# Attention's 1/rms: eleven VectorE operations for two tiles, or a GpSimd power for each tile

## The chip, the cores and the metric

The kernel runs on one core of a Trainium2 chip. Its engines work side by side, each through its own list of instructions in order: TensorE (PE, matrix products and transposes; its weight loads are PEld), VectorE (DVE), ScalarE (ACT), GpSimd (POOL) and SyncE (SP, which only starts DMA transfers). An instruction that needs another engine's result waits at the head of its list, and everything behind it on that engine waits too. The metric is the device time of one execution in microseconds (us): 1328.89 in the median of three runs of the kernel before.

## The reference

Three stages in a row, all in float32, on 8 batches of 576 tokens (4608 in all) and 512 features (8 heads of 64).

```python
kv  = einsum('bhsd,bhse->bhde', k, v)                  # 64 x 64 for each batch and head
out = einsum('bhsd,bhde->bhse', q, kv)
rms = sqrt(mean(out * out, axis=-1, keepdims=True) + 1e-06)   # over the 64 of one head
x   = out / rms * g_norm                               # tokens x 512

h = x @ w_in;   x = (h * cos(h)) @ w_out               # 512 -> 2048 -> 512

h = x @ w_in2                                          # 512 -> 1024
e = exp(h - max(h));  solu = h * e / (sum(e) + 1e-09)
ln = (solu - mean(solu)) / sqrt(var(solu) + 1e-06) * g_ln
out = ln @ w_out2                                      # 1024 -> 512
```

## The kernel before

**Stages.** Attention is cut into 36 tiles of 128 tokens by 512 features. It runs inside the first of four passes over the first feed-forward block: each pass takes 4 of the 16 chunks of 128 hidden features, and goes through 9 blocks of 512 tokens, so a pass has 36 steps. A step multiplies a block of x by one chunk of `w_in` (bank ps_h, lines 174 to 176 from `step_h`), applies h times cos(h) on ACT and DVE, and multiplies by a chunk of `w_out` (banks ps_acc, the same three lines from `step_out`). Each product is done as three products of rounded high and low parts. After the four passes comes the second block. The weights arrive as words of 64 bits and are brought into float32 on the chip (`convert`, `split_w`: lines 500 to 527), most of that on DVE.

**One attention tile.** PE multiplies q by kv (line 416, `first`); ACT squares the result (line 421); DVE sums the squares over each head to 128 x 8 numbers (line 422). Once both tiles of a pair have their sums, DVE makes 1/rms of all 16 columns in eleven small operations (`newton`: a first guess from the bits of the number, then three Newton steps; lines 429 to 440). DVE scales each tile by it (line 458, below called the norm), PE turns the tile by four transposes (line 463, below the turn), and ACT copies the turned tile to x with g_norm (line 469). The products k by v (lines 358 and 360) for the next batches stand between these. The first of a pair's norms therefore waits for the second tile's product, square and sum.

**Order.** The program isn't run in the order in which it is written. `Flow` records every operation as a task with an engine, a duration in us written into the source, the tiles it reads and writes, and a wished time `at`; `run` then plans the engines' lists from these. An engine takes the task with the least `at` among those that could start first; tasks of POOL, and those of DVE that don't have `ps=True`, are planned one at a time (`port`). So another duration or another engine for one task moves others on every engine. The tasks after an attention product have `at` lowered by `PRI`, 20 us, and so go ahead of others when they are ready.

**Other POOL work.** POOL makes the low parts of x (line 569, from block 3 on; DVE does the first three blocks) and of the weights of the later passes (line 527; DVE does those of the first), and in the last stage a power of one column for each tile (line 756):

```python
add("POOL", 0.56, lambda: POOL.tensor_tensor(out=sm("ry"), in0=sm("v"), in1=buf["mhalf"][:, 0:1], op=ALU.pow),
```

Of the kernel before, what the change touches and what calls it, by code (L numbers as in the profile page):

```python
# [10 lines left out]
I32 = mybir.dt.int32  # L11
# [30 lines left out]
MAGIC = float(0x5F3759DF)  # L42

TINY = 0.17
# [18 lines left out]
class Flow:  # L63
# [13 lines left out]
    def declare(self, pool, tag, n, shape, dt=F32):  # L77

        for key in [(tag, i) for i in range(n)] if n else [tag]:
            self.pool_of[key] = pool  # L80
            self.specs.setdefault(pool, []).append((key, shape, dt))
# [18 lines left out]
    def add(self, eng, dur, fn, r=(), w=(), at=0.0, lat=0.0, ps=False):  # L100
        t = Task()
        t.eng, t.dur, t.fn, t.at, t.lat = eng, dur, fn, at, lat
        t.port = eng == "POOL" or (eng == "DVE" and not ps)
# [52 lines left out]
def tile_kernel(ctx, tc, qkv, tail, g2, w1, w2, gl, out):  # L156
# [33 lines left out]
    declare("const", "mhalf", 0, [P, 1])  # L190
# [29 lines left out]
    for n in ("ss", "y", "yt"):  # L220
        declare("att", n, 2, [P, 2 * H])
# [104 lines left out]
    def stage():  # L326
        n_st[0] += 1
        return "st", (n_st[0] - 1) % NST
# [64 lines left out]
    def tile_slots(g):  # L393


        i = g % 2
        bks = [next_bank() for _ in range(2)]
        ss, y, yt = ("ss", i), ("y", i), ("yt", i)
        halves = [("ssh", g, h) for h in range(2)]

        def heads(ap):
            return ap.rearrange("p (n w) -> p n w", w=D)

        def first(h, at):
            t, bk, sq = 2 * g + h, bks[h], stage()
            for b, a, n, row in parts(t):
# [6 lines left out]
                def mm(b=b, a=a, n=n, row=row, qs=qs, kvf=kvf):  # L413
                    for p in range(NPAIR):
# [6 lines left out]
            add("ACT", 0.61, lambda: ACT.activation(out=buf[sq], in_=buf[bk], func=AF.Square), r=[bk], w=[sq], at=at)  # L421
            add("DVE", 0.66, lambda: DVE.tensor_reduce(out=buf[ss][:, h * H:(h + 1) * H], in_=heads(buf[sq]), axis=AX.X,
                                                       op=ALU.add), r=[sq] + ([ss] if h else []),
                w=[halves[h]] + ([] if h else [ss]), at=at)


        def newton(at):
            def start():
                DVE.tensor_scalar(out=buf[ss], in0=buf[ss], scalar1=1.0 / D, scalar2=1e-6, op0=ALU.mult, op1=ALU.add)
                DVE.tensor_scalar(out=buf[y].bitcast(I32), in0=buf[ss].bitcast(I32), scalar1=-0.5, scalar2=MAGIC,  # L430
                                  op0=ALU.mult, op1=ALU.add)

            def square():
                DVE.tensor_tensor(out=buf[yt], in0=buf[y], in1=buf[y], op=ALU.mult)  # L434

            def times():
                DVE.scalar_tensor_tensor(out=buf[yt], in0=buf[yt], scalar=-0.5, in1=buf[ss], op0=ALU.mult, op1=ALU.mult)  # L437

            def update():
                DVE.scalar_tensor_tensor(out=buf[y], in0=buf[yt], scalar=1.5, in1=buf[y], op0=ALU.add, op1=ALU.mult)  # L440

            def all_():
                start()
                for _ in range(3):
                    square()
                    times()
                    update()

            add("DVE", 11 * TINY, all_, r=[*halves, ss], w=[ss, y, yt], at=at)

        def second_(h, at):
            t, bk, xn = 2 * g + h, bks[h], ("xn", h)
# [4 lines left out]
            def norm():  # L457
                DVE.tensor_tensor(out=heads(buf[xn]), in0=heads(buf[bk]),
                                  in1=buf[y][:, h * H:(h + 1) * H].unsqueeze(2).to_broadcast([P, H, D]), op=ALU.mult)
# [7 lines left out]
            add("DVE", 0.71, norm, r=[bk, y], w=[xn], at=at, ps=True)  # L467
# [4 lines left out]
        def run0(at):  # L472
            first(0, at)

        def run1(at):
            first(1, at)
            newton(at - PRI)
            for h in range(2):
                second_(h, at - PRI)

        return [run0, run1]
# [382 lines left out]
    def slot(ps_, c):  # L864
        return ps_ % 2 * CPP + c
# [134 lines left out]
```

## Time and profile before

| | |
|---|---|
| three runs | 1328.19, 1328.89, 1331.12 us; median 1328.89 |
| the profiled execution | 1329.38 us; 1327.6 us from its first to its last instruction |
| busy over that span | PE 98%, DVE 70%, ACT 51%, POOL 29% |
| granted TensorE clock, mean | 0.992 |

The profile is one execution. In its rows a line such as L463 is line 463 of the kernel; an operation is written out<-in by the tiles' names, without buffer numbers; "x4" is four instructions merged, and a merged row's time runs from the first start to the last end. What stands in brackets at a row's end is idle time of the engine before it, and the operation that ended it. PE's busy time holds overlapping matmuls whose ends are modelled. A matmul on float32 operands (lines 358, 360 and 416) shows as two instructions in the trace, and as one in the listings of the program's order.

### The profile page before, as it was taken

How to read it: one execution, taken by the hardware profiler on the slowest of the kernel's cores; microseconds unless marked ns; L12 is line 12 of the kernel's file. 1: busy time of each engine (PE TensorE's matmuls, PEld its weight loads, DVE VectorE, ACT ScalarE, POOL GpSimd, SP SyncE). 2: the span in 40 equal slices, each digit the busy share in tenths (PEclk: the TensorE clock that was granted, in tenths of full speed). 3: DMA queues.
4: the chain of work that ended last, by engine and by line, in shares of the span. 5: the costliest groups of instructions: out<-in, count | busy, mean ns of one | idle time of the engine just before them, and what ended most of it. 6: DMA issues, size and time to landing. Idle time of an engine off the chain costs nothing.

```text
span 1327.6 us, 17232 instructions
## 1 busy us (share of the span) xinstructions
PE 1295.1 (98%) x6148; PEld 1077.8 (81%) x6148; DVE 927.8 (70%) x1620; ACT 676.7 (51%) x1195; POOL 385.6 (29%) x364
## 2 busy tenths in 40 slices
PE   6789899999999999999999999999999999999998
PEld 6678788888888888888888888888788888888886
DVE  5889556588986456754545677878987878787853
ACT  3556445467655445545444555555554544444432
POOL 0001212036663225523131456443232212121100
PEclk9899999999999999999999999999999999999999
DMA  8643244323544243423232535464110111010000
GB/s 299 206 140 115 84 147 131 101 96 96 171 146 135 72 119 113 149 68 123 79 112 87 151 109 159 142 213 137 67 46 35 56 56 46 35 56 25 16 32 32
DMA packets 61830, 139.54 MB, mean 105 GB/s; under 512 B 7344, under 2 KB 9392, under 8 KB 60592
## 3 DMA queue, kind: packets, MB, share of 16 engines
q1 hardware_dynamic: 61744, 138.44, 32.4%
q8 instruction: 48, 0.79, 0.2%
q14 instruction: 38, 0.31, 0.1%
HBM read 91.23 MB, written 47.19 MB: 104 GB/s over the span
## 4 chain that ended last, share of the span: by engine, by line
PE 86%; DVE 6%; DMA 3%; ACT 2%; issue 1%; SPq 0%; POOL 0%; ACTq 0%; DVEq 0%
PE ps_acc L176 13%; PE ps_acc L174 13%; PE ps_acc L175 13%; PE ps_h L174 13%; PE ps_h L176 12%; PE ps_h L175 12%; PE ps_acc L773 2%; PE ps_o L416 2%; PE ps_o L358 2%; DMA xt<-w 2%; PE ps_o L463 1%; DVE att L440 1%; DVE att L437 1%; DVE att L434 1%; DMA xt<-qkv 1%
## 5 line engine op out<-in xcount | busy, mean ns | idle before, releaser
L569 POOL TENSOR_TENSOR xhl<-xt,xhl 128x512 fp32r<-128x512 f32 (+3 forms) x176 | 191.6, 1118 | 360.1 <-ACT xhl L564 359.9
L174 PE MATMUL ps_acc<-temps,wpool 128*128 128x512 f32 x648 | 254.5, 393 | 0.0
L176 PE MATMUL ps_acc<-temps,wpool 128*128 128x512 f32 x648 | 252.5, 390 | 0.0
L175 PE MATMUL ps_acc<-temps,wpool 128*128 128x512 f32 x648 | 252.5, 390 | 0.0
L174 PE MATMUL ps_h<-xhl,wpool 128*128 128x512 f32 x576 | 227.0, 394 | 0.5 <-ACT xhl L564 0.3
L175 PE MATMUL ps_h<-xhl,wpool 128*128 128x512 f32 x576 | 224.6, 390 | 0.2 <-DVE xhl L569 0.2
L176 PE MATMUL ps_h<-xhl,wpool 128*128 128x512 f32 x576 | 224.5, 390 | 0.0
L594 DVE SCALAR_TENSOR_TENSOR temps<-ps_h,temps 128x512 f32<-128x512 f32 x144 | 99.1, 688 | 112.3 <-ACT temps L592 111.8
L603 DVE TENSOR_TENSOR temps<-temps,temps 128x512 fp32r<-128x512 f32 x144 | 122.1, 848 | 69.7 <-ACT temps L602 69.0
L597 ACT ACTIVATE temps<-temps,const 128x512 f32<-128x512 f32 x144 | 104.2, 724 | 94.4 <-DVE temps L594 94.2
L592 ACT ACTIVATE temps<-ps_h 128x512 int32<-128x512 f32 x144 | 85.8, 596 | 129.0 <-PE ps_h L176 128.1
L600 DVE TENSOR_TENSOR temps<-ps_h,temps 128x512 f32<-128x512 f32 x144 | 99.0, 687 | 65.5 <-ACT temps L597 65.3
L176 PEld LDWEIGHTS ps_acc<-temps,wpool 128*128 128x128 f32 x648 | 121.8, 188 | 25.5
L174 PEld LDWEIGHTS ps_acc<-temps,wpool 128*128 128x128 f32 x648 | 122.0, 188 | 24.9 <-DVE temps L630 0.3
L175 PEld LDWEIGHTS ps_acc<-temps,wpool 128*128 128x128 f32 x648 | 121.9, 188 | 24.6
L602 ACT CAST temps<-temps 128x512 fp32r<-128x512 f32 x144 | 89.4, 621 | 100.2 <-DVE temps L600 90.9
L174 PEld LDWEIGHTS ps_h<-xhl,wpool 128*128 128x128 f32 x576 | 108.3, 188 | 23.4 <-issue 0.7
L176 PEld LDWEIGHTS ps_h<-xhl,wpool 128*128 128x128 f32 x576 | 108.2, 188 | 22.6
L175 PEld LDWEIGHTS ps_h<-xhl,wpool 128*128 128x128 f32 x576 | 108.4, 188 | 22.2 <-DVE xhl L569 0.5
L564 ACT CAST xhl<-xt 128x512 fp32r<-128x512 f32 (+3 forms) x192 | 90.8, 512 | 12.8 <-PE ps_h L176 11.9
L756 POOL TENSOR_TENSOR xt<-xt,const 128x1 f32<-128x1 f32 x36 | 23.0, 638 | 196.8 <-DVE xt L753 189.3
L779 DVE TENSOR_TENSOR wpool<-ps_acc,wpool 128x512 fp32r<-128x512 f32 x72 | 46.6, 686 | 42.6 <-ACT wpool L776 42.6
(140 smaller groups left out, 2259.2 us busy)
## 6 DMA issues: line engine op xcount, KB each, us to landing
px<-temps SPq DMA_DIRECT2D x144, 256.0 KB, 2.6
temps<-px SPq DMA_DIRECT2D x108, 256.0 KB, 3.9
xt<-w SPq DMA_DIRECT2D x28, 512.0 KB, 3.9
att<-qkv SPq DMA_DIRECT2D x24, 512.0 KB, 4.7
rawp<-w SPq DMA_DIRECT2D x20, 512.0 KB, 3.8
xt<-px SPq DMA_DIRECT2D x9, 1024.0 KB, 5.1
out<-temps SPq DMA_DIRECT2D x36, 256.0 KB, 2.0
att<-qkv SPq DMA_DIRECT2D x28, 288.0 KB, 5.3
```

Source lines behind the costliest of these rows:

```text
L174: PE.matmul(ps, lhsT=lh, rhs=rh, start=start, stop=False)
L175: PE.matmul(ps, lhsT=lh, rhs=rl, start=False, stop=False)
L176: PE.matmul(ps, lhsT=ll, rhs=rh, start=False, stop=stop)
L564: ACT.copy(out=buf["xh", i][:, k, a - m * TB:a - m * TB + n], in_=xt(k, a, n))
L569: eng.tensor_tensor(out=buf["xl", i][:, k, r], in0=xt(k, a, n), in1=f(buf["xh", i][:, k, r]), op=ALU.subtract)
L592: add("ACT", 0.61, lambda: ACT.activation(out=buf["kk"], in_=h(), func=AF.Copy, scale=INV_2PI, bias=0.25), r=[hb], w=["kk"], at=at)
L594: add("DVE", 0.71, lambda: DVE.scalar_tensor_tensor(out=buf[tk], in0=h(), scalar=INV_2PI, in1=buf["kk"], op0=ALU.mult, op1=ALU.subtract), ...
L597: add("ACT", 0.74, lambda: ACT.activation(out=buf[tk], in_=buf[tk], func=AF.Sin, bias=buf["halfpi"][:, 0:1], scale=2 * math.pi), r=[tk, "h ...
L600: add("DVE", 0.71, lambda: DVE.tensor_tensor(out=buf[tk], in0=h(), in1=buf[tk], op=ALU.mult), r=[hb, tk], w=[tk], at=at, ps=True)
L602: add("ACT", 0.64, lambda: ACT.copy(out=buf[ghk], in_=buf[tk]), r=[tk], w=[ghk], at=at + 2)
L603: add("DVE", 0.71, lambda: DVE.tensor_tensor(out=buf[glk], in0=buf[tk], in1=f(buf[ghk]), op=ALU.subtract), r=[tk, ghk], w=[glk], at=at + 2)
L779: DVE.tensor_tensor(out=buf["ll", n][:, part, :], in0=tr(), in1=f(buf["lh", n][:, part, :]), op=ALU.subtract)
```

## The change

1/rms is made tile by tile, on POOL, by two instructions on 128 x 8 numbers: the sum of squares plus 1e-6, and that to the power -0.5 (a tensor of -0.5 as exponent, `mhalf`, now with 8 columns). The division by 64 goes into the square's scale on ACT. The buffers `ss` and `y` are four of 8 columns instead of two of 16, `yt` goes. A tile's task `rms` is planned with 2.0 us on POOL and outside the one-at-a-time rule; a tile's norm and turn now depend on that tile alone. Lines further down move up by up to 21: the turn is line 443 after the change, the norm 438, the sum 419, the q by kv products 412, the two POOL instructions 426 and 427.

```diff
--- before.py
+++ after.py
@@ -39,9 +39,8 @@
 XP = NT // NX
 
 INV_2PI = float(1.0 / (2.0 * math.pi))
-MAGIC = float(0x5F3759DF)
-
-TINY = 0.17
+
+POW = 2.0
 
 
 
@@ -100,7 +99,7 @@
     def add(self, eng, dur, fn, r=(), w=(), at=0.0, lat=0.0, ps=False):
         t = Task()
         t.eng, t.dur, t.fn, t.at, t.lat = eng, dur, fn, at, lat
-        t.port = eng == "POOL" or (eng == "DVE" and not ps)
+        t.port = eng in ("POOL", "DVE") and not ps
         t.deps, t.next, t.end, t.left, t.seq = set(), [], None, 0, len(self.tasks)
         for k in {*r, *(self.pool_of[k] for k in (*r, *w) if k in self.pool_of)}:
             if k in self.writer:
@@ -187,7 +186,7 @@
     px2 = dram.tile([NB, P, KC, TB], F32, name="px2")
     for key in ("g2", "halfpi"):
         declare("const", key, 0, [P, 1])
-    declare("const", "mhalf", 0, [P, 1])
+    declare("const", "mhalf", 0, [P, H])
     declare("const", "gl", 0, [P, NC])
     declare("const", "ident", 0, [P, P])
 
@@ -217,8 +216,8 @@
         declare(pool, "q" + i, n_q, [P, S])
     declare("att", "kvf", 2, [P, DM])
     declare("att", "xn", 2, [P, DM])
-    for n in ("ss", "y", "yt"):
-        declare("att", n, 2, [P, 2 * H])
+    for n in ("ss", "y"):
+        declare("att", n, 4, [P, H])
 
     for pool, i, n_st, n_y, n_f in (("spare1", "a", 2, 2, 2), ("rawp", "b", 2, 2, 2), ("late_x0", "c", 1, 1, 6)):
         declare(pool, "wst" + i, n_st, [P, 512, 2], U32)
@@ -393,16 +392,13 @@
     def tile_slots(g):
 
 
-        i = g % 2
         bks = [next_bank() for _ in range(2)]
-        ss, y, yt = ("ss", i), ("y", i), ("yt", i)
-        halves = [("ssh", g, h) for h in range(2)]
 
         def heads(ap):
             return ap.rearrange("p (n w) -> p n w", w=D)
 
         def first(h, at):
-            t, bk, sq = 2 * g + h, bks[h], stage()
+            t, i, bk, sq = 2 * g + h, (2 * g + h) % 4, bks[h], stage()
             for b, a, n, row in parts(t):
                 qs = [key("q", b * NPAIR + p, 6, 3) for p in range(NPAIR)]
                 kvf = ("kvf", b % 2)
@@ -418,45 +414,29 @@
 
                 add("PE", 0.89, mm, r=[kvf, ("kvfh", kvf, 0), ("kvfh", kvf, 1), *qs], w=[bk], at=at)
             at -= PRI
-            add("ACT", 0.61, lambda: ACT.activation(out=buf[sq], in_=buf[bk], func=AF.Square), r=[bk], w=[sq], at=at)
-            add("DVE", 0.66, lambda: DVE.tensor_reduce(out=buf[ss][:, h * H:(h + 1) * H], in_=heads(buf[sq]), axis=AX.X,
-                                                       op=ALU.add), r=[sq] + ([ss] if h else []),
-                w=[halves[h]] + ([] if h else [ss]), at=at)
-
-
-        def newton(at):
-            def start():
-                DVE.tensor_scalar(out=buf[ss], in0=buf[ss], scalar1=1.0 / D, scalar2=1e-6, op0=ALU.mult, op1=ALU.add)
-                DVE.tensor_scalar(out=buf[y].bitcast(I32), in0=buf[ss].bitcast(I32), scalar1=-0.5, scalar2=MAGIC,
-                                  op0=ALU.mult, op1=ALU.add)
-
-            def square():
-                DVE.tensor_tensor(out=buf[yt], in0=buf[y], in1=buf[y], op=ALU.mult)
-
-            def times():
-                DVE.scalar_tensor_tensor(out=buf[yt], in0=buf[yt], scalar=-0.5, in1=buf[ss], op0=ALU.mult, op1=ALU.mult)
-
-            def update():
-                DVE.scalar_tensor_tensor(out=buf[y], in0=buf[yt], scalar=1.5, in1=buf[y], op0=ALU.add, op1=ALU.mult)
-
-            def all_():
-                start()
-                for _ in range(3):
-                    square()
-                    times()
-                    update()
-
-            add("DVE", 11 * TINY, all_, r=[*halves, ss], w=[ss, y, yt], at=at)
+            add("ACT", 0.61, lambda: ACT.activation(out=buf[sq], in_=buf[bk], func=AF.Square, scale=D ** -0.5),
+                r=[bk], w=[sq], at=at)
+            add("DVE", 0.66, lambda: DVE.tensor_reduce(out=buf["ss", i], in_=heads(buf[sq]), axis=AX.X, op=ALU.add),
+                r=[sq], w=[("ss", i)], at=at)
+
+        def rms(h, at):
+            i = (2 * g + h) % 4
+
+            def power():
+                POOL.tensor_scalar(out=buf["ss", i], in0=buf["ss", i], scalar1=1e-6, scalar2=None, op0=ALU.add)
+                POOL.tensor_tensor(out=buf["y", i], in0=buf["ss", i], in1=buf["mhalf"], op=ALU.pow)
+
+            add("POOL", POW, power, r=["mhalf"], w=[("ss", i), ("y", i)], at=at, ps=True)
 
         def second_(h, at):
-            t, bk, xn = 2 * g + h, bks[h], ("xn", h)
+            t, i, bk, xn = 2 * g + h, (2 * g + h) % 4, bks[h], ("xn", h)
 
             def tr():
                 return buf[bk].rearrange("p (k n) -> p k n", n=P)
 
             def norm():
                 DVE.tensor_tensor(out=heads(buf[xn]), in0=heads(buf[bk]),
-                                  in1=buf[y][:, h * H:(h + 1) * H].unsqueeze(2).to_broadcast([P, H, D]), op=ALU.mult)
+                                  in1=buf["y", i].unsqueeze(2).to_broadcast([P, H, D]), op=ALU.mult)
 
             def turn():
                 for k in range(KC):
@@ -464,21 +444,20 @@
 
             n, a = divmod(t * P, XP)
             xk = [x for k in range(KC) for x in xkeys(k, t * P, P)]
-            add("DVE", 0.71, norm, r=[bk, y], w=[xn], at=at, ps=True)
+            add("DVE", 0.71, norm, r=[bk, ("y", i)], w=[xn], at=at, ps=True)
             add("PE", 0.42, turn, r=[xn, "ident"], w=[bk], at=at)
             add("ACT", 0.61, lambda: ACT.activation(out=buf[f"xt{n}"][:, :, a:a + P], in_=tr(), func=AF.Copy,
                                                     scale=buf["g2"][:, 0:1]), r=[bk, "g2"], w=xk, at=at)
 
-        def run0(at):
-            first(0, at)
-
-        def run1(at):
-            first(1, at)
-            newton(at - PRI)
-            for h in range(2):
+        def slot(h):
+            def run(at):
+                first(h, at)
+                rms(h, at - PRI)
                 second_(h, at - PRI)
 
-        return [run0, run1]
+            return run
+
+        return [slot(h) for h in range(2)]
 
     def pair_engine(on_dve):
```

Three places in the engines' lists, before and after. (`att_114` and `att_115` are kv, `att_116` and `att_117` the normed tiles, `att_118` on the sums and 1/rms; `temps_97` to `temps_100` the squares; `const_65` the identity of the transposes; `xt_0_86` the weights in conversion. Bank and some other numbers are two higher after the change, since `att` holds two tiles more: `ps_o_137` is `ps_o_135` before.)

PE at the third and fourth pair of tiles (tokens 512 to 1023), behind the first 24 matmuls of `step_h`; before:

```order
L463 MATMUL ps_o_135<-const_65,att_116 128x128 x4
L463 MATMUL ps_o_134<-const_65,att_117 128x128 x4
L416 MATMUL ps_o_135<-att_115,att_112 128x128
L416 MATMUL ps_o_135<-att_115,att_113 128x128
L416 MATMUL ps_o_135<-att_115,xt_0_82 128x128 x2
L416 MATMUL ps_o_134<-att_115,att_112 128x128
L416 MATMUL ps_o_134<-att_115,att_113 128x128
L416 MATMUL ps_o_134<-att_115,xt_0_82 128x128 x2
L463 MATMUL ps_o_135<-const_65,att_116 128x128 x4
L463 MATMUL ps_o_134<-const_65,att_117 128x128 x4
```

and after:

```order
L443 MATMUL ps_o_137<-const_65,att_116 128x128 x4
L412 MATMUL ps_o_137<-att_115,att_112 128x128
L412 MATMUL ps_o_137<-att_115,att_113 128x128
L412 MATMUL ps_o_137<-att_115,xt_0_82 128x128 x2
L443 MATMUL ps_o_136<-const_65,att_117 128x128 x4
L412 MATMUL ps_o_136<-att_115,att_112 128x128
L412 MATMUL ps_o_136<-att_115,att_113 128x128
L412 MATMUL ps_o_136<-att_115,xt_0_82 128x128 x2
L173 MATMUL ps_acc_129<-temps_96,wpool_69 128x512
L174 MATMUL ps_acc_129<-temps_96,wpool_69 128x512
L175 MATMUL ps_acc_129<-temps_96,wpool_69 128x512
L173 MATMUL ps_acc_130<-temps_96,wpool_69 128x512
```

Before, both turns of a pair stand together, then both next products, then both next turns. After, each turn is followed by the product that takes over its bank, and twelve matmuls of the first `step_out` (three of each bank, the first four rows' worth shown) stand ahead of the next turn.

DVE at the third pair, from the middle of its 1/rms; before:

```order
L437 SCALAR_TENSOR_TENSOR att_122<-att_122,att_118 128x16
L440 SCALAR_TENSOR_TENSOR att_120<-att_122,att_120 128x16
L434 TENSOR_TENSOR att_122<-att_120 128x16
L437 SCALAR_TENSOR_TENSOR att_122<-att_122,att_118 128x16
L440 SCALAR_TENSOR_TENSOR att_120<-att_122,att_120 128x16
L434 TENSOR_TENSOR att_122<-att_120 128x16
L437 SCALAR_TENSOR_TENSOR att_122<-att_122,att_118 128x16
L440 SCALAR_TENSOR_TENSOR att_120<-att_122,att_120 128x16
L600 TENSOR_TENSOR temps_95<-ps_h_139,temps_95 128x512
L458 TENSOR_TENSOR att_116<-ps_o_135,att_120 128x512
L458 TENSOR_TENSOR att_117<-ps_o_134,att_120 128x512
L511 SCALAR_TENSOR_TENSOR xt_0_86<-xt_0_86 128x512
```

and after, from that pair's first sum:

```order
L419 TENSOR_REDUCE att_118<-temps_97 128x8
L488 TENSOR_SCALAR xt_0_86<-xt_0_86 128x512
L419 TENSOR_REDUCE att_119<-temps_98 128x8
L490 SCALAR_TENSOR_TENSOR xt_0_86<-xt_0_86 128x512
L573 SCALAR_TENSOR_TENSOR temps_95<-ps_h_141,temps_95 128x512
L438 TENSOR_TENSOR att_116<-ps_o_137,att_122 128x512
L493 TENSOR_TENSOR xt_0_86<-xt_0_86 128x512
L579 TENSOR_TENSOR temps_95<-ps_h_141,temps_95 128x512
L438 TENSOR_TENSOR att_117<-ps_o_136,att_123 128x512
L506 TENSOR_TENSOR wpool_69<-xt_0_86,wpool_69 128x512
L485 SCALAR_TENSOR_TENSOR xt_0_86<-xt_0_86 128x512
L419 TENSOR_REDUCE att_120<-temps_99 128x8
```

The eleven rows of 128x16 are gone; between a sum and its norm now stand rows of the weights' conversion (L488, L490, L493) and of the step (L573, L579), and the two norms of a pair stand apart.

POOL at its first conversions and low parts of x; before:

```order
L527 TENSOR_TENSOR wpool_70<-xt_0_86,wpool_70 128x512 x2
L569 TENSOR_TENSOR xhl_91<-xt_0_78,xhl_91 128x512 x4
L527 TENSOR_TENSOR wpool_70<-xt_0_86,wpool_70 128x512 x2
L569 TENSOR_TENSOR xhl_90<-xt_0_78,xhl_90 128x256
L569 TENSOR_TENSOR xhl_90<-xt_0_82,xhl_90 128x256
```

and after:

```order
L506 TENSOR_TENSOR wpool_70<-xt_0_86,wpool_70 128x512 x2
L426 TENSOR_SCALAR att_121<-att_121 128x8
L427 TENSOR_TENSOR att_125<-att_121,const_63 128x8
L426 TENSOR_SCALAR att_118<-att_118 128x8
L427 TENSOR_TENSOR att_122<-att_118,const_63 128x8
L506 TENSOR_TENSOR wpool_70<-xt_0_86,wpool_70 128x512
L548 TENSOR_TENSOR xhl_91<-xt_0_78,xhl_91 128x512 x2
L426 TENSOR_SCALAR att_119<-att_119 128x8
L427 TENSOR_TENSOR att_123<-att_119,const_63 128x8
L548 TENSOR_TENSOR xhl_91<-xt_0_78,xhl_91 128x512 x2
L506 TENSOR_TENSOR wpool_70<-xt_0_86,wpool_70 128x512
```

Before, these rows follow each other; after, the pairs L426, L427 of the attention tiles stand between them, and thirty such rows stand ahead of this place, where POOL had none before.

## Rows read from the trace of the kernel before

**Rows 1.** Page, part 1: busy us (share of the span) xinstructions.
```profile
PE 1295.1 (98%) x6148; PEld 1077.8 (81%) x6148; DVE 927.8 (70%) x1620; ACT 676.7 (51%) x1195; POOL 385.6 (29%) x364
```

**Rows 2.** Windows: stretch, us; busy PE, PEld, DVE, ACT, POOL (x); PEclk, DMA share, GB/s.
```profile
16.00:60.00 44.00, 31.97 (x202) 28.52 (x202) 38.99 (x100) 24.86 (x42) 0.00 (x0) 0.84 0.68 227
60.00:140.00 80.00, 72.91 (x394) 60.82 (x393) 69.27 (x151) 45.02 (x83) 10.13 (x8) 0.97 0.41 137
140.00:300.00 160.00, 159.14 (x883) 135.29 (x882) 94.22 (x205) 85.37 (x159) 29.28 (x30) 0.99 0.36 115
300.00:800.00 500.00, 500.00 (x2207) 414.01 (x2207) 320.90 (x457) 259.64 (x458) 204.85 (x175) 1.00 0.38 116
```

**Rows 3.** Waits of PE, 0 to 300 us: total, times, longest.
```profile
PE ps_o L463 <- DVE att L458: 9.8, 5, 5.2
...
PE ps_acc L463 <- DVE att L458: 4.0, 1, 4.0
PE ps_o L463 <- ACT wpool L525: 2.7, 1, 2.7
PE ps_o L463 <- ACT temps L602: 2.3, 1, 2.3
```

**Rows 4.** Timeline of DVE, 16 to 60 us: start us, us.
```profile
17.42 0.69 DVE L422 TENSOR_REDUCE att<-temps 128x8 f32<-128x512 f32 x1
...
48.38 0.69 DVE L422 TENSOR_REDUCE att<-temps 128x8 f32<-128x512 f32 x1
...
49.32 0.17 DVE L429 TENSOR_SCALAR att<-att 128x16 f32<-128x16 f32 x1
...
51.41 0.17 DVE L440 SCALAR_TENSOR_TENSOR att<-att,att 128x16 f32<-128x16 f32 x1
...
52.10 1.28 DVE L458 TENSOR_TENSOR att<-ps_o,att 128x512 f32<-128x512 f32 x2
```

**Rows 5.** Timeline of PE, 16 to 60 us; the idle time before it in brackets.
```profile
23.40 1.09 PE L463 MATMUL ps_acc<-const,att 128*128 128x128 f32 x4 [3.97 <-DVE att L458]
24.28 1.92 PE L358 MATMUL ps_o<-att 128*128 128x128 f32 x8
...
28.57 1.06 PE L358 MATMUL ps_o<-xt 128*128 128x128 f32 x8
...
29.68 0.60 PE L463 MATMUL ps_o<-const,att 128*128 128x128 f32 x4
...
46.99 0.72 PE L416 MATMUL ps_o<-att,xt 128*128 128x128 f32 x4
52.94 1.94 PE L463 MATMUL ps_o<-const,att 128*128 128x128 f32 x8 [5.22 <-DVE att L458]
```

**Rows 6.** Groups by line, 0 to 300 us: count | busy, mean ns | idle before.
```profile
L422 DVE TENSOR_REDUCE att<-temps 128x8 f32<-128x512 f32 x36 | 24.6, 684 | 20.3 <-ACT temps L421 20.2
...
L421 ACT ACTIVATE temps<-ps_o 128x512 f32<-128x512 f32 x33 | 19.7, 597 | 11.2 <-PE ps_o L416 10.5 <-ACT att L368 0.2
```

**Rows 7.** POOL at line 756: ns min/median/max.
```profile
L756 POOL TENSOR_TENSOR xt<-xt,const x36: 547/550/1201, 928.1 to 1307.7; 128x1 f32<-128x1 f32 x36
```

**Rows 8.** POOL at line 569: ns min/median/max, with the forms.
```profile
L569 POOL TENSOR_TENSOR xhl<-xt,xhl x176: 449/1282/1817, 127.4 to 869.9; 128x512 fp32r<-128x512 f32 x88, 128x256 fp32r<-128x256 f32 x32, 128x384 fp32r<-128x384 f32 x28, 128x128 fp32r<-128x128 f32 x28
```

**Rows 9.** POOL at line 662: ns min/median/max.
```profile
L662 POOL TENSOR_TENSOR xt<-xt x36: 727/737/1741, 876.2 to 1237.0; 128x256 f32<-128x256 f32 x36
```

**Rows 10.** Timeline of all engines, 132 to 140 us.
```profile
132.45 2.56 POOL L569 TENSOR_TENSOR xhl<-xt,xhl 128x512 fp32r<-128x512 f32 x2 [2.36 <-ACT xhl L564]
132.58 1.20 DVE L440 SCALAR_TENSOR_TENSOR att<-att,att 128x16 f32<-128x16 f32 x1
...
138.89 1.50 PE L463 MATMUL ps_o<-const,att 128*128 128x128 f32 x7 [3.61 <-DVE att L458]
```

**Rows 11.** Timeline of all engines, 1033 to 1037 us.
```profile
1034.36 1.02 DVE L680 TENSOR_TENSOR xhl<-xt,xhl 128x256 fp32r<-128x256 f32 x2
...
1034.53 0.66 POOL L756 TENSOR_TENSOR xt<-xt,const 128x1 f32<-128x1 f32 x1 [5.23 <-DVE xt L753]
```

## The prediction

> **What bounds the kernel now.** I read the page's first part, then windows of stretches, then PE's waits, then the timelines of PE and DVE. PE is busy 1295 us of the span [rows 1], and the windows show where it isn't: from 300 to 800 us it has no gap at all, while it idles 12.0 us of the 44 between 16 and 60 us, 7.1 of the 80 up to 140, and 0.9 in the next 160 [rows 2]. So nothing done to DVE moves the time unless it closes gaps in the first 140 us. There DVE is the busy one: 39.0 of 44 us, then 69.3 of 80. PE's waits name the place: the turn (L463) waits for the norm (L458) 9.8 us and 4.0 us, and two more turns stand behind a conversion's ACT copy and a step's, 2.7 and 2.3 us [rows 3]. I take these two for the same queue: both stand at turns too, and a turn's operand comes from DVE.
>
> Idle time isn't all that is lost. Behind a gap PE runs at the lower of its two levels for some microseconds: eight k by v matmuls take 1.92 us right after the gap that ends at 23.40, and 1.06 us 4 us later [rows 5]. The granted clock says the same, 0.84 and 0.97 of full in the two stretches [rows 2]. Between 1.2 and 2.4 GHz, 0.84 means 14 of the 44 us at the lower level; half of those is lost where PE works, and some lie in the gaps, so I count 6.3 us. Of the 80 us, 0.97 means 4.8, of which 2.4 are lost. To be had at most: 12.0 + 7.1 + 6.3 + 2.4 = 27.8 us.
>
> **What is removed.** One pair's 1/rms on DVE runs from 49.32 to 51.41 + 0.17, 2.26 us [rows 4], and 18 pairs make 41 us of DVE's 928 [rows 1]; half of the pairs come before 140 us. The eleven are also a part of the wait itself. In the gap before 52.94 the products end at 47.71 [rows 5], the sum at 49.07, the eleven operations at 51.58, the norm starts at 52.10 behind one conversion operation, and PE starts 0.84 us after that [rows 4, 5]. From product to turn that is 1.36 to the sum, 0.84 from the norm, and about 3.0 between. Some of the eleven took 1.2 us instead of 0.17, where POOL worked on two 128x512 tensors, and the gap of 3.6 us that follows (a part of the 9.8) goes with them [rows 10].
>
> **What is added.** Per tile an addition and a power on 128x8, on POOL, which does nothing from 16 to 60 us and 10 us of work in the next 80 [rows 2]. The addition: POOL's shortest 128x128 takes 449 ns [rows 8] and its shortest 128x256 727 ns [rows 9], so 2.17 ns a column over a fixed 171; eight columns take about 0.19 us. No row shows a power of eight columns. One column takes 547 ns [rows 7]. If nothing grows with the columns the power stays at 0.55; if each column costs what the first costs above the fixed part, 376 ns, it is 0.17 + 8 x 0.376 = 3.18. With 0.25 for the hand-overs from DVE, between the two and back (estimate, from the 0.16 us between a norm's end, 52.78 by half of its pair, and its turn), the sum s of sum to norm is 1.0 to 3.6 us. I take a power of 1.6, a little under the middle, since a loop over eight columns can share some of what one pays alone: s = 2.0. Only one column is near enough to be measured, so both ends stay in the range.
>
> The plan matters as much as s: the engines' lists are laid out with 2.0 us for this task. In the order after, the work between a product and its turn is what that plan needs. Behind the third pair's first turn PE has a product, a turn, a product and twelve matmuls (500 us hold 2207 [rows 2], so 0.227 each, 2.7 in all) before the next turn, where before it had a turn and two products only. With s = 2.0 the path from product to turn is 1.36 + 2.0 + 0.84 = 4.2 us plus queues.
>
> **The path, step by step, 16 to 60 us.** The first sum is unchanged, 17.42 to 18.11 [rows 4]. Its 1/rms is ready at 20.1; DVE has three more sums and a conversion operation in front, until 21.1, then the norm, 0.68: first turn at 21.85, against 23.40. The four tiles' POOL work queues: the fourth is ready at 18.1 + 4 x 2.0 = 26.1, its turn at about 27.5 against 29.68 [rows 5]. The steps then start 1.5 us earlier. Second gap: by the lists, the product's square stands on ACT behind casts and conversions until about 33.9 (estimate), then come 0.60 for it and 0.68 for the sum [rows 6], s, an interposed step operation and the norm: turn at 38.4. PE, from 30.2, has 24 step matmuls (5.4) and 24 of the products at 0.11 (a fifth less than eight in 1.06 [rows 5], which overlap), 2.7, in front: 38.3. Left is 0.1 of 2.3 us. Third gap: instead of 5.2 us together, waits of 1.05 and 1.5 (each product for the copy of the turned tile out of its bank) and 0.65 (the twelve matmuls for their low part), none at the turns. Then about 0.9, for a conversion that DVE reaches late. With 0.2 and 2.4 at the start (3.97 less 1.55), that makes 6.8 us of idle time for 12.0: 5.2 saved. Of the three half-speed stretches one stays, and I count one short one: 3.1 lost for 6.3, 3.2 saved.
>
> **60 to 140 us.** In the same way each turn has some 5 us of other PE work between its product and itself, so I leave 2.5 of the 7.1 us, and 0.9 of the 2.4: 6.1 saved. **After 140 us** PE waits 0.9 us in all [rows 2], so its turns have a little slack, half a microsecond by estimate; two POOL tensors of 1.28 us [rows 8] can stand in front of an addition, which I charge 1.0. **After 300 us** nothing of this reaches. Sum: 5.2 + 3.2 + 6.1 - 1.0 = 13.5. Against the profiled execution, 1329.4 (its span and 1.8 us around it, which stay), it gives 1315.9; that execution lies 0.5 above the median of the runs, so 1315.4 there. I say 1316.
>
> Costed at nothing: the scale in the square (the same ACT operation), four small buffers instead of two (they remove a wait, if any), seven more columns of a constant. The weights' loads are issued in another place of SP's list, two of them earlier; SP is in order, and one that waits for a buffer holds the k and v loads behind it. Its cover is the two to three tiles that are loaded ahead; gone, it is the third rival.
>
> **A rule against this change.** DVE and POOL do get in each other's way: a 0.17 us operation took 1.20 us beside a POOL tensor [rows 10]. But the power of one column, started within a pair of two-input DVE operations of 256 and 512 columns, took 0.66 us instead of 0.55, and the pair its 1.02 us, which is what their columns take [rows 11]. So the power waited, and DVE didn't. The Trainium skill (SBUF — State Buffer, section on the two separate sides) says that the port pair shared by DVE and GpSimd is an exclusive lock, held for the whole instruction by whoever starts first, and that the other blocks fully. The rows on the plain tensor agree with it and those on the power don't show it; for eight columns no row decides, so it is the second rival.
>
> **Rivals.** (1) *The power is slow.* At 3.18 us, s is 3.6, 1.6 over what the lists are laid out for. At the start the four tiles' POOL work ends at 32.5 instead of 26.1, and the steps start some 4 us later than before, not 1.5 earlier. The turns of a later pair, whose two chains overlap, stand late by 1.6 less 0.5 of slack, so 1.1 for each of the 16 other pairs, 17.6 us. 13.5 - 5.5 - 17.6 = -9.6: 9.6 us slower than before, 1339. With x for the excess over 2.0, the loss is 3.4x + 16(x - 0.5), which eats the gain at x = 1.1: a power of about 2.7. For it: the cost of one column is mostly not fixed cost. Against: a column of a plain tensor costs 2 ns [rows 8, 9], so little of the 376 need recur with each column. (2) *The power holds DVE up.* Fifteen tiles' powers stand before POOL's first tensor; if each stops DVE for 1.0 of its 1.6 us while conversions are next, 15 us of the 20 that DVE gained before 140 us go back, and two thirds of the gain: 1325. (3) *The weights come late.* DVE free, conversions wait for their loads, which wait for the two staging buffers; PE's gaps change their name and half the gain stays: 1322. For it: the DMA share is 0.68 up to 60 us; against: it is 0.41 from 60 to 140 [rows 2]. (4) *The power is quick*, 0.55 to 1.0: the first turns come 1 us and the later ones up to 0.8 us sooner in places where they still wait: 1313.
>
> **Numbers.** Forecast 0.56 (1309 to 1322), quick power 0.10, weights 0.11, DVE held up 0.11, slow power 0.12. A measurement of this kernel can tell 0.2%, 2.7 us, from no change, so faster means under 1326.2. Faster: 0.56 + 0.10, 0.10 of the third rival, 0.06 of the second: 0.82; slower: 0.10 of the first; the rest, 0.08, within. The range of 8 in 10 leaves out the slow power above 1330 and what lies under 1309: 1309 to 1330.
>
> **What would show it.** In the changed profile: the addition and the power of line 426 and 427 at about 0.2 and 1.6 us (over 2.7: rival 1); PE idle under 11 us between 16 and 140 us, with the gap before the third pair's turns and the one near 139 us gone; DVE's busy time down by 40 to 50 us with its two-input operations at their 0.68 us (stretched beside line 427: rival 2); the first turn at about 21.9. Conversions' ACT copies waiting for loads of w before 100 us would be rival 3. The forecast is wrong if PE's waits for the norm stay above 8 us, or if gaps open after 140 us, where I allow one microsecond.

## The result and the profile after

The changed kernel takes 1308.5 us (median of four runs, 1308.1 to 1309.5) against 1329.0 for the one before in the same runs: ratio 0.9849, 95% interval 0.9837 to 0.9861, so 20 us or 1.5% faster. That is the side that was forecast, but half as much again as the forecast gain, and half a microsecond under the low end of the range. The profiled execution took 1308.1 us with a span of 1306.3, against a span of 1327.6.

The first part of the page answers to [rows 1]: DVE is 41.7 us less busy, POOL 73.8 more, PE 8.6 less with the same 6148 matmuls.

```profile
PE 1286.5 (98%) x6148; PEld 1072.4 (82%) x6148; DVE 886.1 (68%) x1422; ACT 679.6 (52%) x1195; POOL 459.4 (35%) x436
```

The windows by stretch, with the columns of [rows 2]:

```profile
16.00:60.00 44.00, 37.48 (x254) 33.70 (x255) 37.17 (x64) 30.20 (x53) 18.47 (x18) 0.96 0.81 273
60.00:140.00 80.00, 79.37 (x458) 67.58 (x458) 60.59 (x99) 49.36 (x90) 36.66 (x32) 1.00 0.43 141
140.00:300.00 160.00, 160.00 (x860) 135.63 (x859) 85.54 (x119) 94.57 (x171) 74.87 (x71) 1.00 0.37 116
300.00:800.00 500.00, 499.88 (x2206) 413.45 (x2205) 313.64 (x456) 256.21 (x451) 199.70 (x172) 1.00 0.39 117
```

PE idles 6.5 us instead of 12.0 in the first stretch, 0.6 instead of 7.1 in the second, and nothing instead of 0.9 in the third; the granted clock goes from 0.84 to 0.96 and from 0.97 to 1.00. The difference lies here: of the 21.3 us of span, 12.95 are idle time before 300 us (behind it PE idles 0.25 us more than before) and 8.6 are busy time. With the number of matmuls unchanged, I put the busy time down to the clock; below it is worked out by stretch.

PE's waits from 0 to 300 us (total, times, longest) answer to [rows 3]. All waits of a turn (now line 443) for its norm (line 438) were 13.8 us there and are 3.3 here; both waits of a turn for ACT are gone. The largest is now the wait for the first products' transfers (5.7 us before).

```profile
PE ps_acc L357 <- DMA att<-qkv: 6.4, 2, 5.0
PE ps_acc L443 <- DVE att L438: 3.3, 2, 2.4
PE ps_o L412 <- ACT xt L449: 1.7, 2, 0.9
```

The addition and the power on POOL (ns min/median/max, first and last start):

```profile
L426 POOL TENSOR_SCALAR att<-att x36: 240/246/892, 19.2 to 255.2; 128x8 f32<-128x8 f32 x36
L427 POOL TENSOR_TENSOR att<-att,const x36: 1667/1667/1953, 19.5 to 255.5; 128x8 f32<-128x8 f32 x36
```

PE's timeline from 22 to 30 and from 40 to 50 us, where [rows 5] had its gaps of 3.97 and 5.22 us (idle time before in brackets):

```profile
22.88 0.63 PE L443 MATMUL ps_acc<-const,att 128*128 128x128 f32 x4 [2.43 <-DVE att L438]
24.41 0.63 PE L443 MATMUL ps_acc<-const,att 128*128 128x128 f32 x4 [0.91 <-DVE att L438]
24.88 1.62 PE L357 MATMUL ps_o<-att 128*128 128x128 f32 x8
...
27.57 1.55 PE L357 MATMUL ps_o<-att 128*128 128x128 f32 x8
...
41.53 0.71 PE L412 MATMUL ps_o<-att,att 128*128 128x128 f32 x4 [0.89 <-ACT xt L449]
...
43.95 0.71 PE L412 MATMUL ps_o<-att,att 128*128 128x128 f32 x4 [0.83 <-ACT xt L449]
...
47.70 0.60 PE L443 MATMUL ps_o<-const,att 128*128 128x128 f32 x4
49.12 1.05 PE L357 MATMUL ps_o<-att 128*128 128x128 f32 x7 [0.82 <-ACT xt L449]
```

No turn of the third pair waits any more; three waits under a microsecond for the turned tile's copy remain. The turn at 47.70, four transposes, takes 0.60 us, the higher level; at 23.40 before the change it took 1.09 [rows 5].

### The profile page after: what moved, and what is told of

The parts are those of the page before. It is cut to its first block, busy times and chain, and to the rows that moved or that the text cites. A ratio compares the mean times of both kernels' runs of the same rounds, so it can differ in the third digit from the quotient of the medians.

```text
span 1306.3 us, 17124 instructions
## 1 busy us (share of the span) xinstructions
PE 1286.5 (98%) x6148; PEld 1072.4 (82%) x6148; DVE 886.1 (68%) x1422; ACT 679.6 (52%) x1195; POOL 459.4 (35%) x436
## 4 chain that ended last, share of the span: by engine, by line
PE 92%; DVE 3%; DMA 1%; ACT 1%; issue 1%; POOL 1%; SPq 0%; ACTq 0%; DVEq 0%
PE ps_acc L175 14%; PE ps_acc L173 14%; PE ps_acc L174 14%; PE ps_h L173 14%; PE ps_h L175 14%; PE ps_h L174 14%; PE ps_acc L752 2%; PE ps_o L412 2%; PE ps_o L357 2%; DMA att<-qkv 1%; PE ps_o L443 1%; POOL att L427 1%; PE ps_acc L357 0%; PE ps_o L359 0%; DMA xt<-w 0%
## 5 line engine op out<-in xcount | busy, mean ns | idle before, releaser
L573 DVE SCALAR_TENSOR_TENSOR temps<-ps_h,temps 128x512 f32<-128x512 f32 x144 | 99.2, 689 | 135.3 <-ACT temps L571 135.0
L579 DVE TENSOR_TENSOR temps<-ps_h,temps 128x512 f32<-128x512 f32 x144 | 99.0, 688 | 60.7 <-ACT temps L576 60.5
L174 PEld LDWEIGHTS ps_h<-xhl,wpool 128*128 128x128 f32 x576 | 108.3, 188 | 21.3
```

Of the source, the lines that this page charges most:

```text
L174: PE.matmul(ps, lhsT=lh, rhs=rl, start=False, stop=False)
L573: add("DVE", 0.71, lambda: DVE.scalar_tensor_tensor(out=buf[tk], in0=h(), scalar=INV_2PI, in1=buf["kk"], op0=ALU.mult, op1=ALU.subtract), ...
L579: add("DVE", 0.71, lambda: DVE.tensor_tensor(out=buf[tk], in0=h(), in1=buf[tk], op=ALU.mult), r=[hb, tk], w=[tk], at=at, ps=True)
```

## The experiments

Every run is compared with the kernel before on the same chip (medians 1328.6 to 1329.0 us). Differences from the changed kernel are from its 1308.5. Whatever alters a task's engine, time or dependences also gives the engines new lists, so a run shows its edit together with its lists; only in *power_twice* do the lists stay as they were.

**What DVE's eleven operations cost, and what the pair.** *dve_load* is the changed kernel with the eleven small operations put back on DVE (planned at 0.205 us each), on buffers that nothing reads; *pair_gate* makes each norm wait for both tiles' powers again, as the pair did before.

```diff
 dve_load (core)
+            add("DVE", 11 * TINY, all_, r=[("ssh", g, 0), ("ssh", g, 1)], w=[ss, y, yt], at=at)
 pair_gate
-            add("DVE", 0.71, norm, r=[bk, ("y", i)], w=[xn], at=at, ps=True)
+            add("DVE", 0.71, norm, r=[bk, ("y", 2 * g % 4), ("y", (2 * g + 1) % 4)], w=[xn], at=at, ps=True)
...
-                second_(h, at - PRI)
+                if h:
+                    for n in range(2):
+                        second_(n, at - PRI)
```

> The changed kernel with the eleven small VectorE operations back, on buffers of their own that nothing reads: per pair, once both sums are there. The norms still take 1/rms from POOL, tile by tile. It gives DVE back its 41 us and leaves the path from product to turn alone. Theory A (the gain is DVE's freed queue: conversions and step operations are reached sooner): most of the gain goes, 1318 to 1327 us, and PE's idle time between 16 and 140 us is back over 13 us. Rival B (the gain is the path: no wait for the partner tile, no eleven operations between sum and norm): 1312 or less.

> The changed kernel, but both norms of a pair wait for both tiles' powers and both turns are listed behind the second product, as before the change. The work on every engine stays. Theory A (DVE's freed queue): 1308 to 1313 us. Rival B (tile by tile is what pays): the first tile's turn comes some 2 us later in each of 18 pairs, and at least half the gain goes: 1318 or more.

Measured: *dve_load* 1318.4 (0.9924 [0.9909, 0.9939]), 10 us of the gain lost: the low end of what theory A gave, with 12.3 us of idle time between 16 and 140 us where A wanted over 13. *pair_gate* 1310.3 (0.9868 [0.9851, 0.9884]), 1.8 lost, which the two spreads hardly separate; rival B's 1318 is refuted. PE's windows and its waits in *dve_load*, then POOL's and DVE's timeline there:

```profile
16.00:60.00 44.00, 33.23 (x208) 29.65 (x207) 37.88 (x97) 24.76 (x42) 15.67 (x16) 0.84 0.70 229
60.00:140.00 80.00, 78.47 (x453) 66.89 (x452) 66.96 (x155) 48.55 (x89) 31.26 (x29) 1.00 0.50 165
```

```profile
PE ps_o L464 <- DVE att L459: 9.8, 4, 4.6
```

```profile
47.69 1.67 POOL L431 TENSOR_TENSOR att<-att,const 128x8 f32<-128x8 f32 x1
...
48.86 0.17 DVE L439 TENSOR_SCALAR att<-att 128x16 f32<-128x16 f32 x1
...
50.95 0.17 DVE L448 SCALAR_TENSOR_TENSOR att<-att,att 128x16 f32<-128x16 f32 x1
51.05 1.28 DVE L459 TENSOR_TENSOR att<-ps_o,att 128x512 f32<-128x512 f32 x2
```

The norm at 51.05 needs none of the eleven: its power ends at 49.36. It stands behind them on an engine in order, which holds it back by 1.7 us, and the turn behind it has its gap of 4.6 us back. The 1.7 us are not the whole gap. From the start of this tile's sum to its turn PE has 1.0 us of work in *dve_load* and 3.7 in the changed kernel (added up from the two traces), because the lists that are planned with the eleven put less in between. So the eleven operations in DVE's queue, with the lists that come of them, are worth about half of the gain, and the early norm of one tile little.

**The same early norm without POOL.** *newton_tile* makes the eleven operations per tile on DVE, in the power's place.

```diff
 newton_tile (core)
-            add("POOL", POW, power, r=["mhalf"], w=[("ss", i), ("y", i)], at=at, ps=True)
+            add("DVE", 11 * TINY, all_, w=[ss, y, yt], at=at)
```

> The changed kernel with the eleven operations on DVE again, tile by tile on 8 columns, and planned with what they take (0.205 us each); POOL makes no power. DVE then has 81 us of them instead of the 41 before the change. Theory A: slower than before the change, 1335 to 1350 us. Rival B: the tile no longer waits for its partner, and the path is no longer than with the power (2.26 against 2.2 us), so faster than before, 1312 to 1322.

Measured: 1334.1 (1.0044 [1.0029, 1.0059]), slower than before, 0.9 us under theory A's range; rival B is refuted. One group of its small operations, 0 to 300 us (busy us, mean ns), and its second window:

```profile
L437 DVE TENSOR_TENSOR att<-att 128x8 f32<-128x8 f32 x108 | 20.0, 186 | 3.7
```

```profile
60.00:140.00 80.00, 70.49 (x370) 56.74 (x368) 73.03 (x208) 43.93 (x83) 5.15 (x4) 0.98 0.42 137
```

Half the columns don't make the operation half as long: in the median 166 ns on 8 columns, 174 on 16. Twice as many of them take 74.5 us of DVE where the kernel before spent 47.0 (the 41 of the prediction and what POOL stretched), and PE idles 9.5 of the 80 us, 7.1 before. Working by the tile, with the operations still on DVE, gains nothing.

**What a slower power costs, by the lists and by itself.** *power_twice* makes each power twice and leaves the planned 2.0 us; *power_twice_planned* also plans the 3.75 us that this takes. *plan_1us*, *plan_2_2us*, *plan_2_5us* and *plan_3us* are the changed kernel with the planned time alone altered; *newton_planned* is the kernel before with its small operations planned at 0.205 us, their distance from start to start, instead of 0.17.

```diff
 power_twice
+                for _ in range(2):
-                POOL.tensor_tensor(out=buf["y", i], in0=buf["ss", i], in1=buf["mhalf"], op=ALU.pow)
+                    POOL.tensor_tensor(out=buf["y", i], in0=buf["ss", i], in1=buf["mhalf"], op=ALU.pow)
 power_twice_planned: that, and
-POW = 2.0
+POW = 3.75
 newton_planned
-TINY = 0.17
+TINY = 0.205
```

> The changed kernel with each power made twice, one after the other, into the same buffer; the plan still reserves 2.0 us, so the engines' lists stay as they are. From sum to norm it takes some 1.75 us more in every tile. By the prediction's formula (3.4 us at the start per us, and 16 pairs late by the excess less half a microsecond) 1308 + 6 + 20 = 1334 us. If the turns have more slack than that (the trace after shows no wait of a turn from 25 us on): 1313 to 1320.

> As the run before with each power made twice, but the plan reserves 3.75 us for a tile's task, near what it takes, so the engines' lists are laid out anew. Rival C (what counts is that the plan's duration and the real one agree; the lists are laid out so that a turn comes just when the plan has its tile ready): most of the 49 us goes, 1309 to 1320 us. If the longer path itself costs them: 1335 or more.

> The changed kernel with the plan's duration for a tile's task 1.0 instead of 2.0 us; the same instructions in another order. Rival C: each turn is listed 1 us too early, and by the 28 us per us that the doubled power showed (49 for 1.75), about 1336 us. If the duration in the plan matters little: 1308 to 1313.

> The changed kernel planned with 2.2 us, which is nearer to what the trace after shows from the end of a sum to the end of its power (0.25 + 1.67 and two hand-overs of 0.08, so 2.1). If agreement is all: 1306 to 1309 us. If each plan is a draw of its own around the same value: 1308 to 1313.

> As the run before, planned with 2.5 us: half a microsecond of spare time at each turn. If spare time helps: 1305 to 1308 us; if 2.0 is near the best: 1309 to 1313, as with 3.0.

> The changed kernel planned with 3.0 us instead of 2.0. Rival C: turns are listed a microsecond later than needed, which costs little as PE has other work: 1306 to 1312 us. If the order at 2.0 is good by itself and not by the agreement: 1315 or more.

> The kernel before, with the plan's duration for each of the eleven operations 0.205 us, which they take from start to start, instead of 0.17: 2.26 us for a pair instead of 1.87. Rival C (a part of the gain is only that the plan now agrees with the chip): 0.39 us over 18 pairs at the price that the doubled power showed, 5 to 6 us faster than before, 1321 to 1325. Theory A (DVE's queue): 1327 to 1331.

| kernel | us | ratio to before, 95% interval | to after, us |
|---|---|---|---|
| power_twice | 1357.4 | 1.0217 [1.0202, 1.0233] | +48.9 |
| power_twice_planned | 1313.9 | 0.9889 [0.9874, 0.9905] | +5.4 |
| plan_1us | 1332.3 | 1.0024 [1.0015, 1.0034] | +23.9 |
| plan_2_2us | 1308.8 | 0.9855 [0.9840, 0.9870] | +0.3 |
| plan_2_5us | 1309.5 | 0.9861 [0.9846, 0.9876] | +1.1 |
| plan_3us | 1313.0 | 0.9881 [0.9860, 0.9902] | +4.6 |
| newton_planned | 1328.1 | 0.9992 [0.9982, 1.0002] | |

*power_twice* lies above both of its forecasts. *plan_1us*, *power_twice_planned* and *newton_planned* came out where one of theirs has them: near 1336, in 1309 to 1320 and in 1327 to 1331. *plan_2_2us* lies in both ranges and decides nothing between them; *plan_2_5us* lies in the range without a gain from spare time; *plan_3us* falls between its two, and its runs spread from 1310.8 to 1315.8.

PE's waits for norms from 0 to 300 us in *power_twice*, then in *plan_1us*:

```profile
PE ps_o L444 <- DVE att L439: 34.2, 28, 2.2
PE ps_acc L444 <- DVE att L439: 6.6, 3, 3.4
```

```profile
PE ps_o L443 <- DVE att L438: 17.4, 21, 3.6
PE ps_acc L443 <- DVE att L438: 4.5, 3, 1.6
```

The third window (140 to 300 us) of *power_twice*, of *plan_1us* and of *power_twice_planned*, where PE had no gap after the change:

```profile
140.00:300.00 160.00, 140.81 (x785) 116.82 (x783) 60.17 (x90) 75.16 (x138) 87.11 (x78) 1.00 0.33 107
```

```profile
140.00:300.00 160.00, 152.48 (x831) 126.55 (x830) 70.86 (x105) 84.79 (x154) 66.59 (x68) 1.00 0.32 104
```

```profile
140.00:300.00 160.00, 160.00 (x868) 135.63 (x867) 81.53 (x117) 92.05 (x169) 104.23 (x90) 1.00 0.33 107
```

*plan_1us* has the instructions of the changed kernel, each as long as there, and loses more than the whole gain: its lists put less of PE's other work in front of a turn (3.4 us from the start of a tile's sum to its turn, in the median of the 36 tiles, against 4.4 after the change; added up from the traces), and there are 24 waits for norms where the changed kernel has two. The doubled power loses 49 us if the lists don't know of it and 5 if they do. From 2.0 to 2.5 the time is flat. That the lists agree with the measured time isn't a gain in itself: for the kernel before it gives nothing that can be told from no change (*newton_planned*). What all these runs fit is that PE's other work has to stand between product and turn, and enough of it for the time that the path really takes.

**The power for a pair at once, and the shared port.** *power_pair* sums both tiles into one buffer and makes one addition and power of 16 columns, planned at 3.4 us. *port_counted* lets the lists treat the addition and power like other POOL work, which they keep apart from DVE's work on the on-chip memory.

```diff
 power_pair (core)
-            add("POOL", POW, power, r=["mhalf"], w=[("ss", i), ("y", i)], at=at, ps=True)
+            add("POOL", POW, power, r=["mhalf", ("ssh", g, 0), ("ssh", g, 1)], w=[("ss", i), ("y", i)], at=at, ps=True)
 port_counted
-            add("POOL", POW, power, r=["mhalf"], w=[("ss", i), ("y", i)], at=at, ps=True)
+            add("POOL", POW, power, r=["mhalf"], w=[("ss", i), ("y", i)], at=at)
```

> The changed kernel with one power of 16 columns for a pair, once both sums are there, planned with 3.4 us. One column took 547 ns and eight 1667, so 160 ns a column more: 2.95 us for sixteen. POOL does the 18 instead of 36 additions and powers. If, as the run with the norms of a pair gated showed, waiting for the partner costs little: 1309 to 1315 us. If the longer path to the first norm of a pair counts (3.3 instead of 2.0 us, planned): 1316 to 1322.

> The changed kernel with the task of a tile's 1/rms planned as every other of POOL, never at the same time as a DVE operation on SBUF alone. The instructions are the same; the plan then keeps 2.0 us free of such DVE operations around each power. The trace after shows DVE operations beside the power at their usual 0.68 us, so the plan would keep free what needs no keeping: 1312 to 1325 us, slower than the changed kernel. If the power did hold DVE up: 1308 or less.

Measured: *power_pair* 1317.6 (0.9916 [0.9899, 0.9932]), 9.1 behind the change by the tile; *port_counted* 1314.9 (0.9898 [0.9883, 0.9912]), 6.4 behind. The power in *power_pair* (ns min/median/max), then PE's waits for norms in *port_counted*:

```profile
L430 POOL TENSOR_TENSOR att<-att,const x18: 2929/2932/3242, 20.4 to 273.0; 128x16 f32<-128x16 f32 x18
```

```profile
PE ps_o L443 <- DVE att L438: 6.0, 3, 4.8
```

*power_pair* lies in the range of the longer path, *port_counted* in that of a plan which keeps free what needs no keeping. One power of 16 columns is 0.4 us shorter than two of eight, but it starts only after the second sum and is itself 1.27 us longer than one of eight; which of these, or the new lists, costs the 9.1 us no run separates. In the lists that keep DVE away from a running power a turn waits 4.8 us, and DVE needs no such protection, as this timeline of the changed kernel shows. First POOL and then DVE from 36.8 to 41 us, then the same from 60.4 to 64:

```profile
36.82 0.34 POOL L426 TENSOR_SCALAR att<-att 128x8 f32<-128x8 f32 x1 [9.23 <-DVE att L419]
37.25 1.67 POOL L427 TENSOR_TENSOR att<-att,const 128x8 f32<-128x8 f32 x1
...
39.32 1.67 POOL L427 TENSOR_TENSOR att<-att,const 128x8 f32<-128x8 f32 x1
```

```profile
37.57 0.69 DVE L490 SCALAR_TENSOR_TENSOR xt<-xt 128x512 f32<-128x512 uint32 x1
...
39.55 0.68 DVE L493 TENSOR_TENSOR xt<-xt 128x512 f32<-128x512 f32 x1
```

```profile
60.86 0.61 POOL L426 TENSOR_SCALAR att<-att 128x8 f32<-128x8 f32 x1 [1.60 <-DVE att L419]
61.55 1.94 POOL L427 TENSOR_TENSOR att<-att,const 128x8 f32<-128x8 f32 x1
```

```profile
60.69 1.89 DVE L548 TENSOR_TENSOR xhl<-xt,xhl 128x512 fp32r<-128x512 f32 x3
```

Both DVE operations read two inputs from on-chip memory, start and end within a power, and keep their 0.68 to 0.69 us. Three more at 60.69 take 0.63 us each from start to start, and it is the addition and the power beside them that grow, from 0.24 to 0.61 and from 1.67 to 1.94. Of the 27 such DVE operations before 300 us that meet no POOL work but an addition or a power, none takes more than 0.69 us, as with POOL idle; beside POOL's other tensors some take up to 1.80 (read from the trace of the changed kernel, operation by operation).

## Why the prediction was right in direction and too small

- **The power** was taken at 1.6 and measures 1.67, the addition 0.19 and 0.25. The choice between 0.55 and 3.18 came out well, by luck: no row had the cost of a further column, which is 0.16 us, between the 0 and 0.376 that made the bounds. Rivals 1 and 4 fall with it. With hand-overs s is about 2.1, near the 2.0 of the lists.
- **16 to 60 us.** Idle time was to fall to 6.8 and fell to 6.5. The first turn came at 22.9, not 21.9, because the first sum started 1 us later in this run (PE waited 0.7 us longer for the first transfers, and eight k by v matmuls behind them took 1.65 us for 1.16); from that sum (18.43) to the turn it is 4.45 us, 4.43 in the working. The gap before the third pair's turns is gone. Two waits for copies, 0.89 and 0.83 us, take its place, for 1.05 and 1.5 in the working; the 0.65 of the twelve matmuls didn't come. That the sum agrees so well is in part luck: the second turn's wait of 0.91 and the copy's 0.82 at 49.12 weren't in it, and the conversion's 0.9 that was didn't come.
- **The failed step** is what was left over after 60 us: "I leave 2.5 of the 7.1 us" (0.6 stayed) and the charge of 1.0 after 140 us (0.9 was gained instead). That is 3.8 us. The working itself had found some 5 us of other PE work between a product and its turn against 4.2 needed, and then left a third of the gaps standing on no row. *plan_1us* and *power_twice* show that such gaps come back where s is longer than the lists have it. The two parts aren't equally firm. The 0.9 after 140 us is gained in *plan_2_2us*, *plan_2_5us*, *plan_3us* and *pair_gate* too (PE busy all 160 us). How much stays from 60 to 140 us depends on the lists: *plan_2_2us*, as fast at 1308.8, idles 2.2 us there, about what I left, and 5.1 us from 16 to 60 instead of 6.5. The 0.6 is this list's own.
- **The clock** is the other mis-sized term. 4.7 us were to come back, 8.6 did. I kept 3.1 us lost up to 60 us (one long and one short half-speed stretch) and 0.9 after it, and put nothing on the 0.99 of the third stretch [rows 2], where the half-speed stretch behind the gap that ends at 138.89 [rows 10] goes on past 140 us. The first window is of the kernel before, the other four are of the changed kernel around its gaps:

```profile
140.00:145.00 5.00, 5.00 (x29) 4.62 (x28) 1.41 (x3) 2.22 (x4) 0.00 (x0) 0.72 0.14 26
```

```profile
22.80:26.50 3.70, 2.71 (x17) 2.54 (x18) 3.62 (x7) 1.90 (x3) 3.37 (x5) 0.82 1.01 350
26.50:29.20 2.70, 2.70 (x17) 2.70 (x17) 2.22 (x5) 0.69 (x1) 1.09 (x1) 0.61 0.07 21
40.00:49.00 9.00, 6.58 (x41) 5.32 (x39) 8.06 (x14) 5.84 (x12) 5.19 (x5) 1.00 0.82 280
49.00:52.00 3.00, 2.88 (x25) 2.88 (x26) 3.00 (x7) 2.69 (x6) 0.00 (x0) 1.00 0.25 42
```

 Read as a share between 1.2 and 2.4 GHz, 0.72 of 5.0 us is 2.8 us at the lower level, 1.4 lost, which came back uncounted. 0.82 of 3.7 us and 0.61 of 2.7 are 1.3 and 2.1 us at the lower level, so 1.7 stayed lost for 3.1, and nothing for 0.9. That is 3.7 of the 3.9. The one stretch that stays comes behind two gaps, of 2.43 and 0.91 us, in which PE stood still for 3.34 of 3.96 us; the first turn after the longer one still took 0.63 us. From 40 us on, behind 0.89, 0.83 and 0.82 us, the clock stays at 1.00. The two mis-sized terms and 0.3 from the first stretch make 8.0 us (1.9 + 1.9 + 3.9 + 0.3), which with 13.5 is the 21.3 of the span within 0.2.
- **Rival 1's price** was too low though its case didn't come. For an excess of 1.75 us it gives 3.4 x 1.75 + 16 x 1.25 = 26; *power_twice* lost 49. I charged one wait for each pair less half a microsecond; 31 turns of 36 waited, 40.8 us in all, so nearly every tile's turn is late, not one of each pair.
- **Rival 2** (the power holds DVE up) is refuted by the rows at 37.57 and 39.55: beside the power they take what they take alone. The Trainium skill (SBUF — State Buffer, section on the two separate sides) would have a DVE operation with two inputs from that memory and a POOL operation that reads it block each other, the later one for the other's whole instruction. For this power the trace doesn't show it: the two run side by side, and even the longest power beside such operations, 1.95 us, is only 0.29 us longer than the shortest. *port_counted*, whose lists keep all DVE work on that memory apart from the power, is 6.4 us slower.
- **Rival 3** (late weights): from 16 to 140 us ACT waited 5.3 us for loads of w before the change (longest 1.9) and waits 1.2 us after it (longest 0.5), so the loads didn't come to limit it.
- **What stays open.** *dve_load* puts the eleven back and keeps 10 of the 20 us. That the kept half is the power's place on POOL, started by each tile's sum while DVE does other work, is inferred; no run isolates it, nor the four buffers in place of two. The parts needn't add up either, since each kernel has lists of its own.

## What to carry to other kernels

Where lists are laid out ahead from planned times, plan a task on a waiting chain at about what it measures, hand-overs included: 1.0 us planned for 2.1 cost 24 us here, 2.5 planned cost about 1. A right time alone is no gain (*newton_planned*). Small operations on a busy engine in order cost by where they stand, not only by their sum: eleven of 0.17 us held a norm back by 1.7 us that didn't need them. When counting what a change leaves over, compare the path with the work that covers it, place by place, and leave over only what that comparison leaves.

## What the runs showed of the hardware that was not expected

- POOL's power takes 550 ns for one column [rows 7], 1667 for eight, 2932 for 16 (medians): about 0.16 us for each column more, and about 0.39 fixed.
- A running power left DVE's two-input operations at 0.69 us; when the two met, the power (up to 1.95 us for 1.67) and the addition (up to 0.89 for 0.24) were longer than alone, while a plain POOL tensor stretched a DVE operation from 0.17 to 1.20 us [rows 10].
- Small DVE operations take 166 ns on 128x8 (*newton_tile*) and 174 to 175 on 128x16 (the kernel before), in the median: half the columns save 5%.
- Gaps of 0.82 to 0.89 us on PE left the granted clock at 1.00. In *plan_2_2us* one gap of 2.43 us before the first turn was followed by 0.51 in the mean of the three microseconds from 22 us on; in *plan_2_5us* a gap of 3.16 us at the same place left it at 1.00, behind products that had in part run at the lower level (24 in 4.42 us, 2.94 in the changed kernel). So the length of the gap alone doesn't tell.
